# Sliding-window attention into soft-MoE on one core: masks and value order moved to TensorE, 128-key tiles with halos, longer weight rows

## The chip, the cores and the metric

One core of one Trainium2 chip. The metric is the time of one execution on the device in microseconds, the median of the runs. Everything that is called busy, waiting or a clock below is read from the profiles of single executions; the span of a profile is about 1.8 us shorter than the measured time of the same run. "Full" and "half" clock are the two rates that the clock records of the TensorE show (1.00 and 0.50).

## The reference, cut to what matters

```python
# q, k, v: (8 batches, 8 heads, 576 tokens, 64), fp32
scores = q @ k.T / 8
rel = pos[:, None] - pos[None, :]
mask_plain = (rel >= 0) & (rel < 32)                        # heads 0..3
mask_dil   = (rel >= 0) & (rel < 128) & (rel % 4 == 0)      # heads 4..7
attn = softmax(where(mask, scores, -1e9));  o = attn @ v
x = o.transpose(0, 2, 1, 3).reshape(4608, 512)
logits = x @ phi                                            # phi: 512 x 32 slots
d = softmax(logits, axis=0);  slot_in = d.T @ x             # sums over all 4608 rows
slot_out[e] = relu(slot_in[e] @ w1[e]) @ w2[e]              # 8 experts, 2 + 2 MB each, fp32
out = softmax(logits, axis=1) @ slot_out
```

The sum over all rows splits the work in two. No expert product can start before the last batch's attention is done; the weights can be loaded under the attention.

## The kernel before

Eight batches run in a software pipeline. Each has six score tiles (`kt` 0 to 5): TensorE computes them, ScalarE takes the exponent, VectorE multiplies by a 0/1 mask, and eleven output tiles follow. Values of the plain heads arrive in six overlapping tiles of 96 new keys; dilated heads use tokens sorted by residue modulo 4.

```python
def load_v(b):                       # 128-byte pieces (64 fp16) for the plain heads
    nc.gpsimd.dma_start(out=vt[32:128, :, :, 0:D],
        in_=v[b, 0:4].rearrange("h (t a) d -> a (h t) d", t=NT))
    ...                              # dilated heads: 512-byte rows into a stage, then ScalarE copies

def emit_scores(b, kt):
    ...
    for kt_, k0, qt_, q0, c0, w in jobs:
        for tt in range(2):
            for hh in range(2):
                p0 = 32 * (2 * pair + hh)
                nc.tensor.matmul(sps[:, hh, c0:c0+w], kt_[p0:p0+32, k0:k0+128, tt],
                                 qt_[p0:p0+32, q0:q0+w, tt], start=(tt == 0), stop=(tt == 1))

def emit_mask(b, kt):                # six a batch, on VectorE
    nc.vector.tensor_tensor(out=pt[:, :, 0:n], in0=pt[:, :, 0:n],
        in1=m[:, None, :].broadcast_to([128, 2, n]), op=ALU.mult)
# ... cut: emit_av (11 tiles, two PSUM buffers), transposes of x, logits, slot sums
# after the last batch: hps = siTm x w1 (64 products), hT, so = hTm x w2 (64), 36 output tiles
```

The softmax here doesn't subtract the row's maximum and nothing guards it: scores larger than these inputs give would overflow.

## Time and profile before

| | before |
|---|---|
| median of 4 runs, us | 202.8 (202.54 to 204.49) |
| span of the profile, us | 200.8 |
| TensorE busy, VectorE busy, ScalarE busy, us | 146.6, 132.3, 100.6 |
| first score product of batches 0, 1, 2, 7, us | 9.1, 24.2, 39.2, 126.5 |
| expert products hps from, to; so from, to, us | 156.5, 162.1; 164.4, 170.7 |

These are lines of the page of the profile before. Each digit is the busy share of one fortieth of the span, in tenths (about 5 us each); GB/s is what the DMA engines moved, counted in bytes at the destination (loads as the 2-byte results of 4-byte reads, the output of the tail as 4-byte numbers); the last line is the chain of waits that ended last, by engine.

```profile
span 200.8 us, 5070 instructions
PE   0126369399889989979799998998886869758600
PEclk9999999999999999999999999955555599995555
GB/s 128 182 191 192 205 211 189 209 212 187 211 210 188 214 210 203 196 212 194 204 210 189 208 207 208 207 208 208 207 207 205 70 0 0 127 407 407 410 407 124
PE 41%; DMA 23%; ACT 10%; issue 10%; DVE 7%; POOL 6%; POOLq 0%; ACTq 0%
```

The DMA runs at about 205 GB/s until some 157 us; then the tail moves output at 407 GB/s. The dips to 187 to 194 are single slices. And TensorE is nearly as busy as the DMA from 45 us on. The view by windows has it for 40 to 149 us (columns: window, its length, then busy us and count of PE, PEld, DVE, ACT, POOL, then clock, DMA share, GB/s):

```profile
40.00:149.00 109.00, 98.18 (x1555) 66.96 (x1553) 87.19 (x250) 67.04 (x104) 28.95 (x37) 0.91 1.29 204
```

TensorE works for 98.18 of 109 us, 90%, against 80% for VectorE.

The PEclk row needs care: the records of this execution begin at 126.4 us, and the row prints 9 before that for want of a record. These groups of products by form in one batch (73 to 92.1 us) show the real clock. The columns are line, engine, operation, output and inputs, shapes, count, busy us, mean ns of one, idle time before.

```profile
L360 PE MATMUL lg_0_1329<-xTd_1277,phi_61 128*128 128x288 f16 x2 | 0.8, 418 | 0.0
L342 PE MATMUL rd_0_1629<-ident,xd_1439 128*128 128x128 f16 x5 | 1.1, 303 | 0.0
```

In the same trace the last two of a run of 128-column transposes start 106 or 107 ns apart (those before them 79 to 92), and 96-column ones 79 or 80. That is one column in 0.83 ns, half clock.

### The profile page before, as it was taken

The page shows a single profiled execution, that of the slowest core. Times are in us where ns is not written, and L with a number is a line of the kernel's source. Part 1 is how long each engine was busy: PE and PEld are TensorE (multiplying, and loading weights), DVE is VectorE, ACT ScalarE, POOL GpSimd, SP SyncE. Part 2 cuts the span into 40 slices and gives each one's busy share as a digit, 9 for nine tenths or more (in the row PEclk, how much of TensorE's full clock was granted, in tenths as well). Part 3 has the DMA queues.
Part 4 walks back from the last instruction along what each step waited for, and adds up shares of the span by engine and source line. Part 5 has one row for each costly group of instructions (what it writes and reads, how often), then busy time and mean ns, then how long its engine had stood idle before and what let it go on. Part 6 is the DMA issues. An engine that isn't in the chain of part 4 may idle for free.

```text
span 200.8 us, 5070 instructions
## 1 busy us (share of the span) xinstructions
PE 146.6 (73%) x2128; PEld 91.8 (46%) x2128; DVE 132.3 (66%) x354; ACT 100.6 (50%) x150; POOL 66.9 (33%) x102
## 2 busy tenths in 40 slices
PE   0126369399889989979799998998886869758600
PEld 0115256158647746646465675675655344211000
DVE  3688697678896998597779678986632120755520
ACT  2037448384872963595386675565433020655510
POOL 7736224215215403501750003055000000598850
PEclk9999999999999999999999999955555599995555
DMA  6999999999999999999999999999999400499994
GB/s 128 182 191 192 205 211 189 209 212 187 211 210 188 214 210 203 196 212 194 204 210 189 208 207 208 207 208 208 207 207 205 70 0 0 127 407 407 410 407 124
DMA packets 46422, 40.99 MB, mean 204 GB/s; under 512 B 20672, under 2 KB 33600, under 8 KB 46400
## 3 DMA queue, kind: packets, MB, share of 16 engines
q0 software_dynamic: 46112, 40.41, 117.0%
q8 instruction: 16, 0.26, 0.5%
q1 hardware_dynamic: 288, 0.27, 0.4%
q14 instruction: 6, 0.05, 0.1%
HBM read 62.20 MB, written 9.44 MB: 357 GB/s over the span
## 4 chain that ended last, share of the span: by engine, by line
PE 41%; DMA 23%; ACT 10%; issue 10%; DVE 7%; POOL 6%; POOLq 0%; ACTq 0%
DMA v_93<-in_v_dram 10%; DMA vsa_1638<-in_v_dram 8%; DMA vsa_148<-in_v_dram 5%; PE so L597 3%; POOL out_dram L621 3%; ACT ET L363 3%; PE hps L563 3%; DVE qk_89 L200 1%; ACT v_92 L174 1%; PE lg_0_977 L360 1%; PE s_4_1993 L238 1%; PE lg_0_1329 L360 1%; PE lg_0_2031 L360 1%; PE lg_0_626 L360 1%; POOL raw_0_121 L150 1%
## 5 line engine op out<-in xcount | busy, mean ns | idle before, releaser
L238 PEld LDWEIGHTS <-qk_89 32*128 32x128 f16 x448 | 14.1, 116 | 22.3 <-DVE qk_89 L200 10.5
L238 PEld LDWEIGHTS <-qk_90 32*128 32x128 f16 x448 | 14.4, 113 | 10.3 <-issue 5.1
L621 POOL DMA_DIRECT2D out_dram<-ot_3191 x1 | 0.6, 561 | 33.4 <-ACT ot_3191 L616 33.4
L360 PEld LDWEIGHTS <-phi_61 128*128 128x128 f16 x64 | 7.6, 128 | 8.1 <-issue 3.5
L613 PEld LDWEIGHTS <-ET 128*128 128x128 f16 x36 | 3.6, 99 | 14.3 <-issue 13.0
L238 PE MATMUL s_0_178<-qk_89 32*128 32x96 f16 x12 | 0.7, 270 | 9.1 <-DVE qk_89 L200 9.1
L193 POOL DMA_DIRECT2D w_5_2337<-in_moe_w_dram x1 | 0.9, 873 | 18.0 <-PE o_0_2311 L273 18.0
L580 ACT ACTIVATE h_sb<-hps 128x512 f16<-128x512 f32 x1 | 0.6, 598 | 9.8 <-PE hps L563 9.8
L605 DVE CAST so_sb<-so 128x256 f16<-128x256 f32 x1 | 0.4, 425 | 6.8 <-ACT so_sb L604 6.8
L581 DVE TENSOR_SCALAR h_sb<-hps 128x512 f16<-128x512 f32 x1 | 0.7, 692 | 6.3 <-ACT h_sb L580 6.3
L251 ACT ACTIVATE pa_0_191<-s_0_178 128x576 f16<-128x576 f32 x1 | 0.7, 651 | 7.8 <-PE s_0_178 L238 7.8
L374 PEld LDWEIGHTS <-ET 32*128 32x128 f16 x48 | 1.9, 99 | 5.5 <-ACT ET L363 5.5
L238 PE MATMUL s_2_214<-qk_89 32*128 32x96 f16 (+2 forms) x28 | 1.1, 215 | 4.3 <-DVE qk_89 L209 3.7
L405 PEld LDWEIGHTS <-ones 96*128 96x128 f16 x48 | 4.0, 103 | 0.0
L563 PEld LDWEIGHTS <-siTm 128*32 128x32 f16 x64 | 2.1, 128 | 4.1 <-issue 2.5
L563 PE MATMUL hps<-w_0_76,siTm 128*32 128x512 f16 x8 | 3.2, 548 | 1.0 <-DVE siTm L549 1.0
L193 POOL DMA_DIRECT2D w_7_2689<-in_moe_w_dram x4 | 2.8, 707 | 3.1 <-PE o_0_2663 L273 2.9
L157 POOL DMA_DIRECT2D v_92<-in_v_dram x3 | 3.6, 1195 | 0.7 <-DMA raw_0_121<-in_q_dram 0.7
L200 DVE STREAM_TRANSPOSE qk_89<-raw_0_121 128x576 uint32<-128x576 uint32 x1 | 1.3, 1256 | 3.9 <-DMA raw_0_121<-in_q_dram 3.9
L184 DVE COPY v_93<-v_93 32x1280 f16<-32x1280 f16 x2 | 1.0, 484 | 4.2 <-DMA v_93<-in_v_dram 4.2
L157 POOL DMA_DIRECT2D v_91<-in_v_dram x3 | 3.6, 1209 | 0.0
L391 DVE TENSOR_TENSOR er_2948<-ep_2933,emask 128x352 f16<-128x352 f16 x1 | 0.3, 342 | 4.9 <-PE ep_2933 L384 4.9
(1047 smaller groups left out, 614.0 us busy)
## 6 DMA issues: line engine op xcount, KB each, us to landing
w_0_76<-in_moe_w_dram POOLq DMA_DIRECT2D x1, 1024.0 KB, 18.6
w_1_77<-in_moe_w_dram POOLq DMA_DIRECT2D x1, 1024.0 KB, 18.6
w_2_78<-in_moe_w_dram POOLq DMA_DIRECT2D x1, 1024.0 KB, 14.8
w_3_79<-in_moe_w_dram POOLq DMA_DIRECT2D x1, 1024.0 KB, 13.5
w_4_80<-in_moe_w_dram POOLq DMA_DIRECT2D x1, 1024.0 KB, 17.7
w_5_81<-in_moe_w_dram POOLq DMA_DIRECT2D x1, 1024.0 KB, 16.0
w_6_82<-in_moe_w_dram POOLq DMA_DIRECT2D x1, 1024.0 KB, 13.4
w_7_83<-in_moe_w_dram POOLq DMA_DIRECT2D x1, 1024.0 KB, 18.5
```

The costliest lines, as they stand in the source:

```text
L150: nc.gpsimd.dma_start(out=t[:, g, :], in_=ten[b, 4 * g : 4 * g + 4].rearrange("h (p j) d -> (h p) (j d)", j=PJ),)
L157: nc.gpsimd.dma_start(out=vt[32:128, :, :, 0:D], in_=v[b, 0:4].rearrange("h (t a) d -> a (h t) d", t=NT))
L193: nc.gpsimd.dma_start(out=w2t[e][:, n * i : n * i + n, :], in_=src[:, n * i : n * i + n, :])
L200: nc.vector.transpose(out=dst, in_=src)
L238: nc.tensor.matmul(sps[:, hh, c0 : c0 + w], kt_[p0 : p0 + 32, k0 : k0 + 128, tt], qt_[p0 : p0 + 32, q0 : q0 + w, tt], start=(tt == 0), sto ...
L360: nc.tensor.matmul(lp, phi4[:, kc].rearrange("p c s -> p (c s)"), rhs, start=(kc == 0), stop=(kc == 3))
L363: nc.scalar.activation(out=ET[:, b * S : b * S + S].rearrange("p (i r) -> p r i", r=DIL)[:, 2 * rp : 2 * rp + 2, :], in_=lp, func=AF.Exp, ...
L405: nc.tensor.matmul(up[:, c, :], l, rr, start=(i == 0), stop=(i == len(jobs) - 1), skip_group_check=True)
L563: nc.tensor.matmul(hps[32 * j : 32 * j + 32, fc, :], siTm[:, dc, e, :], w1t[e][:, dc, 512 * fc : 512 * fc + 512], start=(g == 0 and dc == ...
L597: nc.tensor.matmul(so[32 * j : 32 * j + 32, :], hTm[g][:, c, 32 * j : 32 * j + 32], w2t[4 * g + j][:, c, :], start=(g == 0 and c == 0), st ...
L613: nc.tensor.matmul(fp, ET[:, r0 : r0 + 128], so_sb, start=True, stop=True)
L621: nc.gpsimd.dma_start(out=out[r0 : r0 + 128, :], in_=ot)
```

## The change

Its intent is to unload VectorE and ScalarE, to give the DMA longer rows, and to keep the array busy with useful work:

- The mask is added before the exponent: a product of the identity with a bias tile (0 or -30000) opens each score tile. Twelve such products a batch, 5376 columns; the six VectorE mask products go.
- Keys are in tiles of 128, with query windows of 160 (plain) and 144 (dilated). Queries that reach back into the tile before get a second, 32-by-32 product from it, a halo: 32 a batch.
- Values arrive four tokens to a row. One-hot products (24 a batch, 256 columns each) put them in order, and VectorE evicts the result three times a batch. GpSimd copies the values of the dilated heads.
- The values of the last 64 tokens of all batches are loaded in one go at the start (`vleft`).
- Weight rows are 8 KB (w1) and 16 KB (w2) of input instead of 4 KB and 2 KB.
- 24 products on zeros warm the array; the outputs use one PSUM buffer of two banks.

```diff
-def make_masks():   # 0 / 1
+def make_bias():    # 0 / -30000
@@ load_v
-            out=vt[32:128, :, :, 0:D], in_=v[b, 0:4].rearrange("h (t a) d -> a (h t) d", t=NT)
+            out=st, in_=v[b, :, 0:512, :].rearrange("h (a r) d -> a h (r d)", r=DIL)
+    def load_vleft():
+        for b in range(B):
+            nc.gpsimd.dma_start(out=vleft[16 * b : 16 * b + 16],
+                in_=v[b, :, 512:576, :].rearrange("h (a r) d -> a h (r d)", r=DIL))
+    def permute_v(b, part):            # one-hot products, then an eviction
+            for u in range(2):
+                t = 2 * part + u
+                for r in range(DIL):
+                    nc.tensor.matmul(pv[:, u], sel[:, 128 * t + 3 - r : 128 * t + 131 - r],
+                        st[:, 0:4, D * r : D * r + D], start=(r == 0), stop=(r == DIL - 1))
... (part 2: the same for vleft)
+        nc.vector.tensor_copy(out=dst, in_=pv)
@@ load_w1, load_w2
-  moe_w1[e].rearrange("(c p) f -> p c f", p=128)
+  moe_w1[e].rearrange("(g p c) f -> p g (c f)", g=2, c=2)
-  moe_w2[e].rearrange("(c p) f -> p c f", p=128)
+  moe_w2[e].rearrange("(p c) f -> p c f", c=8)
@@ emit_scores
+        for hh in range(2):
+            nc.tensor.matmul(sps[:, hh, 0:n] ..., ident, <bias tile>, start=True, stop=False)
... (then the score products with start=False)
-    def emit_mask(b, kt): ...
@@ emit_av: two output tiles a group, products "mains" of 128 keys, then "halos"
+                        halos.append((slice(o0, o0 + 32), h, hl, vp[96:128, u - 1, h]))
+            jobs = mains + halos
... (cut: strides of the transposes of x, warm-up, the order of loads)
+N_WARM = 24
```

## The prediction

> **What bounds the kernel now.** Loads. The table of slices shows the DMA over 90% busy from 5 to 155 us at 187 to 214 GB/s of 2-byte results (62.2 MB are read as 4-byte numbers, so about twice that), and the last weight lands near 157 us. Behind it comes a serial tail: in the chain of waits the expert products hps run 156.5 to 162.1, so 164.4 to 170.7, then 36 stores at 407 GB/s; the span ends at 200.8, so 30.1 us after so. Attention takes about 17 us a batch (the first score products of batches 3 to 7 start at 57, 73, 90, 107 and 126 us) and ends at 154.4, level with the loads.
>
> **A hidden cost: the matrix clock.** The table prints clock 1.00 until 126 us, but that is only a lack of records. In the timeline 128-column transposes start 106 ns apart and 65-column products 54 ns apart: half clock, by the two rates that the Trainium skill gives (TensorE: Matmul & The Clock Gate, "Wait — 56ns, not 53.3ns?": 107 against 56 ns). From 160.5 to 181 us, 512-column products start 215 ns apart: full clock. Adding up columns weighted by the share of array rows and columns used, in the 3.41 us steps of the clock records, I estimate that the clock rose after windows at 0.39 and 0.50 of the full rate and fell after 0.23 and 0.25. Attention averages about 0.27, so it stays at half clock.
>
> **What the change does, per batch.**
> - VectorE loses 6 mask products (0.45 to 0.68 us each) and the value shifts (0.5 + 0.4), merges 11 normalisations into 5, and gains 3 evictions of about 0.7 us: about 15 to 12.5 us.
> - ScalarE loses two 1.05 us copies (one goes to GpSimd), and gains 15% of exponent columns: about 11.5 to 10 us.
> - TensorE gains 12 identity products (5376 columns), 24 one-hot products (some 5400) and 32 small halo products: 240 to 290 products. My estimate of its array time is 11.4 us before at half clock; after, 21 us at half or 10.5 us at full clock. The weighted use after would be 9 us of full rate per batch, 0.6 of a 15 us batch, above what raised the clock. The 24 warm-up products start it high. I expect mostly full clock.
> - DMA: 128-byte value rows become 512-byte ones, weight rows 2 to 8 times longer. The dips to 187 GB/s should nearly go: 6 us less load time. Three fewer first-layer weights go ahead of the last batch's values, so attention may run ahead of the weights.
>
> **Critical path.** If a batch takes 14 to 15 us, attention ends near 140 us, hps leaves the path, and what stays is loads to about 152 us, the last eight so products (3.4 us at half clock), and the unchanged 30 us: 186 us of span, 188 us measured with the 1.8 us by which the median exceeds the span. Each microsecond of batch time above 14.4 delays the loads by about 5 us, since they wait for staging buffers; at 17 us all gain is gone.
>
> **Predicted: 188 us, 182 to 198 (8 in 10). Faster by over 2%: 0.86; within: 0.07; slower: 0.07.**
>
> **What would show it.** Transposes 53 to 60 ns apart and full clock in most attention windows; score starts 14 to 15 us apart; no dips below 200 GB/s; hps finished 5 us or more before the last weight lands; VectorE busy near 110 us.
>
> **What would make it wrong.** The clock falling back (21 us a batch, some 225 us); the two-buffer PSUM ring, now taking 11 tiles a batch instead of 8, or the single output buffer stalling the in-order TensorE; GpSimd's copies holding up load issue, leaving gaps in the DMA rows.

## The result and the profile after

The kernel after takes 211.76 us (median of 4 runs, 211.28 to 212.46) against 202.8 us before. The ratio is 1.0419, with a 95% interval of 1.0368 to 1.0469: slower, outside the predicted range. All ratios here are the mean time of one kernel's fast runs over that of the other's in the same rounds, so they are not quite the ratio of the medians.

The lines of the page after that answer to those of before:

```profile
span 210.1 us, 5705 instructions
PE   7959749989999998998998998998856869768600
PEclk9967979999999999999999999999655599995555
GB/s 107 194 159 161 202 207 209 208 212 209 210 211 207 202 150 208 178 106 204 219 74 210 216 222 218 212 215 218 211 220 201 9 0 3 51 408 409 407 409 113
PE 60%; ACT 11%; DVE 10%; issue 7%; DMA 4%; POOL 4%; POOLq 0%; ACTq 0%
```

How to read the difference: the chain of waits has moved from the DMA (23% to 4%) to TensorE (41% to 60%). VectorE's busy time fell from 132.3 to 106.8 us, TensorE's rose from 146.6 to 172.7 us. The clock record now begins at 5.2 us and is real: full from 32.5 to 148.5 us. The same view by windows as before has TensorE at work for 103.55 of 109 us, 95%:

```profile
40.00:149.00 109.00, 103.55 (x1853) 69.43 (x1850) 62.44 (x124) 68.53 (x95) 23.98 (x33) 1.00 1.05 196
```

Three slices of the GB/s row drop deeply (150, then 178 and 106, then 74).

The starts of the batches' first score products show where the time went (after the change the first product of a score tile is its bias product; lengths are taken before rounding):

| us | before | after | change of the stretch |
|---|---|---|---|
| batch 0 | 9.1 | 8.4 | |
| batch 2 | 39.2 | 49.2 | start: +10.7 |
| batch 7 | 126.5 | 133.3 | five batches: 87.3 to 84.2, -3.1 |
| hps | 156.5 | 165.4 | last batch and drain: 30.0 to 32.0, +2.0 |
| end of the span | 200.8 | 210.1 | tail: 44.3 to 44.7, +0.4 |

A batch fell from 17.5 to 16.8 us, where 14 to 15 had been predicted, and the start lost more than five batches gained. The tail is unchanged, as predicted.

The same groups of products after, in one batch (66.11 to 82.87 us), against the lines of before above: the logits take 286 ns instead of 418, the transposes 222 instead of 303, at the same shapes. In the trace, transposes start 56 ns apart instead of 106. The clock did double. So the matrix clock, rival C below, is not what keeps these batches long.

```profile
L396 PE MATMUL lg<-xT,phi 128*128 128x288 f16 x8 | 1.5, 286 | 0.7 <-ACT xT L383 0.7
L379 PE MATMUL rg<-ident,x 128*128 128x128 f16 x8 | 0.8, 222 | 0.0
```

So why does a batch still take 16.8 us? These are all the waits of TensorE in that batch (view of waits; columns: us in total, times, longest):

```profile
PE lg L396 <- ACT xT L383: 0.7, 1, 0.7
```

TensorE waits for others for 0.7 us of 16.8. It is the bound itself. By start-to-next-start times in this batch, by use, against what I had estimated from the columns alone, with products on different parts of the array taken as overlapping:

| products in a batch | estimate, us at full clock | measured, us |
|---|---|---|
| bias | 2.25 | 2.84 |
| scores | 2.2 | 4.52 |
| probabilities times values, with halos | 1.25 | 2.91 |
| one-hot | 2.25 | 2.71 |
| transposes of x | 1.0 | 1.48 |
| logits | 0.96 | 1.01 |
| slot rows and sums | 0.6 | 1.32 |
| sum | 10.5 | 16.8 |

Of the 6.3 us between the sums, 3.6 are the changes of tile shape that come next, 0.7 is the wait above, and 1.9 lie in products that follow each other less closely than their columns allow, 0.7 of them in the value products with their halos.

This stretch of the timeline shows one reason (start us, busy us, what, count):

```profile
69.61 0.28 PE L342 MATMUL o<-v,pb 128*128 128x65 f16 x4
69.73 0.53 PE L269 MATMUL s<-bias,ident 128*128 128x432 f16 x2
70.19 0.80 PE L285 MATMUL s<-qk 32*64 32x64 f16 x28
```

From four value products to the bias products both use the whole array; the four take 0.12 us, 30 ns each. The two bias products of 432 columns start at 69.73 and need 2 x 182 ns, so they are done streaming at about 70.09; the score products on 32 rows of the array start at 70.19, a tenth of a microsecond later, and nothing is waited for. Over all batches from 49 to 150 us there are 38 such changes of the array's tile shape in a batch. Each costs a median of 96 ns beyond the columns streamed (middle half: 93 to 98 ns), 3.6 us a batch. Where one group of products that use the whole array follows another such group, the median is 12 ns. Before the change there are 27, at a median of 125 ns at half clock.

The Trainium skill says in "TensorEngine Tiling (Array Packing)", section "Key Properties", that changing the tiling mode drains the TensorE. It gives no figure; this trace shows a cost there and puts 96 ns on it, without showing what it is made of.

The halos are the second reason. These are instruction starts from the trace after (us, then ns since the product before), four halos of plain heads and four of dilated ones:

```
71.152 122      71.614 124
71.192  40      71.617   3
71.228  36      71.620   3
71.257  29      71.623   3
```

The four dilated halos use the same 32 rows and four different 32-column places of the array and start 3 ns apart, as the skill has it ("TensorE: Matmul & The Clock Gate", sections "The mechanism" and "Measured speedup vs the span model": tiles at different positions overlap, with starts about 4 ns apart). The sixteen halos of plain heads share one place in each group of four, and follow each other at 29 to 40 ns. I had costed all of them as if they overlapped. By these spacings that is an estimated 0.4 us a batch, much less than the changes of shape; and the first of each group pays such a change.

### The profile page after: what moved, and what is told of

Read it like the earlier page. It is cut to its first block, busy times and chain, and to the rows that moved or that the text cites. A ratio compares the mean times of both kernels' runs of the same rounds, so it can differ in the third digit from the quotient of the medians.

```text
span 210.1 us, 5705 instructions
## 1 busy us (share of the span) xinstructions
PE 172.7 (82%) x2552; PEld 104.4 (50%) x2552; DVE 106.8 (51%) x209; ACT 96.2 (46%) x134; POOL 61.3 (29%) x99
## 4 chain that ended last, share of the span: by engine, by line
PE 60%; ACT 11%; DVE 10%; issue 7%; DMA 4%; POOL 4%; POOLq 0%; ACTq 0%
PE s L285 12%; PE o L342 11%; PE pv L186 8%; ACT xT L383 6%; DMA vs<-in_v_dram 4%; PE s L272 4%; PE lg L396 4%; PE u L444 4%; PE s L269 3%; PE rg L371 3%; PE so L644 3%; POOL out_dram L668 3%; ACT pc L299 3%; PE hps L610 3%; DVE qk L232 2%
## 5 line engine op out<-in xcount | busy, mean ns | idle before, releaser
L285 PE MATMUL s<-qk 32*32 32x16 f16 (+3 forms) x832 | 35.9, 210 | 4.3 <-DVE qk L232 4.1
L285 PEld LDWEIGHTS <-qk 32*128 32x128 f16 (+2 forms) x832 | 22.0, 93 | 26.5 <-issue 19.7
L212 DVE CAST v<-pv 128x512 f16<-128x512 f32 x24 | 16.4, 688 | 28.7 <-PE pv L204 18.0
L174 POOL COPY v<-vs 128x1024 f16<-128x1024 f16 x8 | 8.4, 1046 | 75.7 <-PE o L342 56.8
L668 POOL DMA_DIRECT2D out_dram<-ot x36 | 19.0, 533 | 36.6 <-ACT ot L663 34.6
L352 DVE TENSOR_TENSOR x<-o,rc 128x512 f16<-128x512 f32 x40 | 27.4, 685 | 1.0
L299 ACT ACTIVATE pa<-s 128x960 f16<-128x960 f32 x16 | 15.4, 970 | 25.8 <-PE s L285 25.7
L232 DVE STREAM_TRANSPOSE qk<-raw 128x576 uint32<-128x576 uint32 x16 | 19.3, 1233 | 6.5 <-PE s L285 3.2
L186 PE MATMUL pv<-vs,sel 128*128 128x256 f16 x128 | 19.8, 307 | 2.6 <-DMA vs<-in_v_dram 2.4
L383 ACT COPY xT<-rg 128x512 f16<-128x512 f16 x16 | 20.8, 1310 | 0.2 <-PE rg L382 0.2
L241 DVE STREAM_TRANSPOSE qk<-raw 128x320 uint32<-128x320 uint32 (+1 forms) x32 | 19.7, 662 | 0.3 <-DMA raw<-in_q_dram 0.2
L660 PE MATMUL f<-so_sb,ET 128*128 128x512 f16 x36 | 14.4, 452 | 4.1 <-DVE ot L665 2.1
L272 PE MATMUL s<-bias,ident 128*128 128x480 f16 (+1 forms) x64 | 17.4, 356 | 0.0
```

The lines of the kernel that those rows point to most:

```text
L186: nc.tensor.matmul(pv[:, u], sel[:, 128 * t + 3 - r : 128 * t + 131 - r], st[:, 0:4, D * r : D * r + D], start=(r == 0), stop=(r == DIL - 1),)
L212: nc.vector.tensor_copy(out=dst, in_=pv)
L232: nc.vector.transpose(out=dst, in_=src)
L241: nc.vector.transpose(out=o, in_=i)
L272: nc.tensor.matmul(sps[:, hh, 0:n].rearrange("p (t i) -> p t i", t=3), ident, win[:, None, 0:w].broadcast_to([128, 3, w]), start=True, sto ...
L285: nc.tensor.matmul(sps[m if isinstance(m, slice) else slice(0, m), hh, c0 : c0 + w], l, r, start=False, stop=(tt == 1 and ji == len(jobs) ...
```

## The experiments

Theory A: the batch is bound by one in-order chain on TensorE, and what it costs beyond the columns is the changes of tile shape. Rival B: the loads, held back behind GpSimd's copies (the prediction had named this). Rival C: the matrix clock. All kernels below gave correct results. "Batch" is the time from one batch's first score product to the next.

### Is it TensorE or the loads?

**e1, fewer changes of shape.** Value products of two output tiles are issued first and their halos after them; short transposes and slot sums use all 128 rows.

```diff
-            jobs = mains + halos
-            for i, (ps, h, l, rr) in enumerate(jobs):
-                nc.tensor.matmul(...)
+            allmains += ...;  allhalos += ...
+        for uu, ps, h, l, rr, first, last in allmains + allhalos:
+            nc.tensor.matmul(...)
-            n0 = 64 if u == 4 else 0
+            n0 = 0          # rows 0..63 of that tile weighted by zero
```

> Same work, nine fewer changes of array shape per batch (38 to about 29): the products of both halves of an output group are ordered by shape, and the two transposes and the slot sums of the last 64 tokens use all 128 rows. Theory A (the in-order TensorE binds attention even at full clock, and each change of array shape costs 96 ns, as the trace of the changed kernel shows): 0.86 us less per batch, 6 to 8 us less in all, about 204 to 206 us. Theory B (loads held back by the GpSimd copies bind): no change, 211 us, within 1 us.

Measured 208.38 us, ratio 1.0263 (1.0200 to 1.0325). The changes fell to 29 a batch, and undisturbed batches to 16.2 us from 16.8 (one took 16.5, one 17.0): 0.6 us for nine changes, about 70 ns each where 96 had been reckoned. The whole is 3.4 us less than after, in the direction of A but short of the expected 204 to 206.

**e2, GpSimd's copy behind the loads.**

```diff
-            if att and kt == 2 and b + 1 < B:
-                spread_v_dil(b + 1)
+            if kt == 2 and 0 < b < B - 1:
+                for e in (b,) if b < B - 2 else (b, b + 1):
+                    spread_v_dil(e)
```

> The GpSimd copies of the strided values move behind the loads of two batches ahead, so that loads no longer wait for an output product. Theory B: the gaps in the DMA rows near 73, 90 and 107 us (some 8 us of lost transfer) vanish and the time falls by 5 to 8 us. Theory A: the gaps vanish or shrink, the weights land earlier, but the expert products start as late as before, and the time stays within 1.5 us of 211.8.

Measured 211.21 us, ratio 1.0385 (1.0300 to 1.0471). First what GpSimd's queue waited for after the change, then the GB/s row of e2.

```profile
POOL v L174 <- PE o L342: 56.8, 5, 12.8
```

```profile
GB/s 102 197 161 164 204 207 209 206 215 208 212 209 208 214 207 210 212 210 212 213 218 223 210 218 162 218 213 218 215 104 0 3 0 3 48 408 407 408 409 114
```

After the change the copies wait 56.8 us in total for the output products of TensorE, with the loads queued behind them. In e2 the three deep drops are gone (one slice of 162 is left), and the last weight lands at 156.7 us instead of 164.3. The batch is 16.8 us as before, hps starts at 165.3 instead of 165.4, and the time is within the scatter of after. Rival B is refuted: the gaps are real and cost nothing, because the loads have slack behind TensorE.

**e3, the bias products twice.** The same values are added a second time, which changes no masked result.

```diff
-        for hh in range(2):
+        for rnd, hh in ((0, 0), (0, 1), (1, 0), (1, 1)):
...
-                    start=True,
+                    start=(rnd == 0),
```

> Every identity product of the mask bias is run twice (adding minus 60000 instead of minus 30000; the result is the same). 12 products more per batch, 5376 columns, 2.24 us at full clock, 17.9 us over eight batches. Theory A (TensorE binds): 15 to 18 us more, 227 to 230 us. Theory B (loads bind, TensorE has slack): under 5 us more. The clock should stay full, since the array is used more.

Measured 222.75 us, ratio 1.0929 (1.0835 to 1.1023). The batch grew by 1.7 us to 18.5 us for 2.24 us of added columns, and hps came 11.8 us later, at 177.1. So three quarters of the time added on TensorE lengthened the batch: it is on the path. But the total, 11 us more than after, missed the 227 to 230 of A. (The profile is slow by its time, with the clock full from 41 to 164 us, so the batches are those of full clock.)

### The start

**e4, no warm-up.** One product on zeros instead of 24 (`N_WARM = 1`).

> 1 warm-up product instead of 24. The trace of the changed kernel shows that the full clock it won was lost at 12 us anyway and won again by the attention itself at 18.8 and for good at 32.5 us. So I expect no more than 2 us either way, and the full clock from about 33 us on. If the warm-up is what holds the clock, the attention stays at half clock and the time rises by 30 us or more.

Measured 213.78 us, ratio 1.0520. The clock went full on its own at 17.4 us and held from 34.5 to 150.5 us. The warm-up is worth about 2 us, and is not what holds the clock high.

**e5, the last values with each batch.** `vleft` is loaded per batch, the queries and keys of batch 1 come earlier, and the one-hot products of batch 1 move into batch 1.

```diff
-    load_vleft()
-    nc.gpsimd.dma_start(out=phi_raw, ...)
     load_qk(0, 1)
     load_qk(1, 1)
+    nc.gpsimd.dma_start(out=phi_raw, ...)
@@ in load_v
+        nc.gpsimd.dma_start(out=vleft[b], in_=v[b, :, 512:576, :]...)
-            if b == 0 and kt in (1, 2, 3): permute_v(0, kt - 1)
-                    if b == 0: ... permute_v(1, part)
+            if b == 0 and kt in (2, 3, 4): permute_v(0, kt - 2)
+            if b == 1 and kt < 3: permute_v(1, kt)
```

> Only the start is changed: the values of the last 64 tokens come with each batch instead of all eight batches before batch 1's queries and keys, and the first one-hot products stand later in TensorE's order. In the changed kernel batch 1's first complete scores wait until 29.0 us (24.2 before), and batch 2 starts at 49.2 (39.2 before). Theory: the start costs 5 to 10 us of the loss, since everything after it is one TensorE chain; so batch 2 starts at 40 to 44 us, the batch time stays at 16.8 us, and the whole is 204 to 207 us. If the start is hidden by a later limit: no change, 211 us.

Measured 215.23 us, ratio 1.0549, a clear miss. Batch 1 started at 25.0 us and batch 2 at 51.0 instead of 49.2. The clock was half from 24.6 to 34.9 and from 38.3 to 45.1 us, where after it was half for only 3.4 us in that stretch. The lower clock may have taken what the order gained; no run separates the two.

### Taking work off TensorE

**e6, plain values in order by DMA.** Rows of one token again, so that 16 of 24 one-hot products and two of three evictions go.

```diff
+        for h in range(4):
+            nc.gpsimd.dma_start(out=vP[b % 4][:, :, h, 0:D],
+                in_=v[b, h, 0:512, :].rearrange("(t a) d -> a t d", a=128))
-            out=st, in_=v[b, :, 0:512, :]...
+            out=st, in_=v[b, 4:8, 0:512, :]...
@@ permute_v
-        if part < 2: ... (16 one-hot products)
+        if part < 2: return
```

> The plain heads' values of the first 512 tokens come straight from the DMA in key order, in runs of 64 numbers as before the change, so 16 of the 24 one-hot products and two of three evictions per batch fall away. TensorE theory: 1.75 us less per batch (16 products 109 ns apart), 10 to 13 us in all, 199 to 202 us. DMA theory (short runs are what hurt): the dips of the kernel before come back, loads end later and the time does not fall, or rises.

Measured 210.01 us (207.08 to 215.97), ratio 1.0194 (1.0127 to 1.0261), not the 199 to 202 expected. The profile is slow: batches of 15.4 us at full clock, and of 19.8 and 21.4 us in a stretch from 51.2 to 82.0 us at half clock. The start did gain: batch 2 began at 42.7 us instead of 49.2, with the same wait of 4.0 us for batch 1's queries. The dips to 188 GB/s came back, as the other theory had it, but the last weight landed at 164.0 us, against 164.3 after.

**e7, everything at once.** The edits of e1, e2, e5 and e6, and one strided ScalarE eviction a batch moved to VectorE.

> Fewer shape changes, late copies, the new load order, values by DMA, and one of the two strided evictions of the dilated half on VectorE, all together. TensorE theory: 16.8 - 0.8 - 1.75 - 0.6 gives 13.5 to 14.5 us per batch, batch 2 starts near 41 us, attention ends near 140 us; then the end of the loads (150 to 154 us), the last second-layer products and the 30 us of stores remain: 186 to 192 us, faster than both kernels. If something else binds, it stays above 198 us.

Measured 208.88 us (204.06, 205.75, 212.01, 214.96); fast runs against fast runs 1.0056 (0.9983 to 1.0130). The profile is fast:

```profile
span 202.3 us, 5487 instructions
PE   7929999998999999898998998998757969768600
PEclk9965555698555555999999999999855599995555
```

Batches 4 to 6 take 14.4, 14.4 and 14.2 us, just what the prediction had said, though with 16 one-hot products a batch fewer than it counted, so the agreement is luck. Batches 1 to 3 take 19.7, 21.0 and 19.6 us, in the stretch where PEclk is 5 (half from 11.8 to 39.1 and from 49.3 to 80.0 us). Batch 2 began at 44.1 us. Both stretches run the same program, with TensorE busy 100% of the time at half clock (49.3 to 80.0 us) and 93% at full clock (80.0 to 144.9). So at this amount of work either clock holds itself. My estimate of the use, columns weighted by the share of array rows and columns they occupy, is about 6.8 us of full-rate work a batch: 0.34 of a 20 us batch, 0.47 of a 14.4 us one. In the kernels before and after, a 3.41 us step was followed by full clock when its use was above about 0.39 and by half clock when it was below about 0.35; these two values lie on either side. Counted the same way over all fifteen traces, 240 of 241 steps below 0.35 were followed by half clock and all 468 above 0.42 by full; between the two both occur (95 full, 39 half). Plain columns, not weighted by the share of the array, do not sort the steps like this. The steps are estimates (a few per cent of the product records can be missing), and the rule is a fit, not something the profile prints.

**e8, the kernel before with useless products.** Twelve identity products a batch are written into the score tiles and then overwritten.

```diff
+        for hh in range(2):
+            nc.tensor.matmul(sps[:, hh, 0:n], ident, masks[:, 0:n], start=True, stop=True)
```

> The kernel before, with two useless identity products ahead of each score tile (12 per batch, 4672 columns, overwritten by the scores), only to use the array more. By my threshold estimate the weighted use rises from 0.27 to about 0.4 to 0.45 of full rate, so the clock should rise in most of attention: 128-column transposes 56 ns apart instead of 106. If half clock was a cost to the kernel before, it gets faster by over 2% in spite of the added work; if its loads bound it, it stays within 2%: I expect 199 to 204 us. If the clock does not rise: 210 us or more.

Measured 205.35 us, ratio 1.0065 (1.0018 to 1.0113). Useless work did raise the clock of the old kernel in parts (full from 73.5 to 90.5 and from 131.5 to 148.6 us, among shorter stretches, in a profile that is slow by its time), and in all it bought nothing.

**e9, four of six masks back on VectorE**, as a product after the exponent; only the mixed tiles keep their bias products.

```diff
-            else:
-                nc.tensor.matmul(sps[...], ident, win[...], start=True, stop=False)
+                        start=(kind != 1 and tt == 0),
+    def emit_mask(b, kt):
+            nc.vector.tensor_tensor(out=p4, in0=p4, in1=keep[...], op=ALU.mult)
```

> The changed kernel with the mask of four of the six score tiles per batch (the plain and the first three strided ones) applied on VectorE after the exponential, as before the change, instead of by identity products: 8 products (2688 columns) per batch less for TensorE, 4 products of about 0.6 us more for VectorE. TensorE theory at full clock: 1.1 to 1.5 us less per batch, 15.3 to 15.7 us, 201 to 205 us. But the clock theory warns: the weighted use per batch falls from about 9 to 7.9 us of full rate; at full clock that is 0.5 of a batch, above the 0.38 at which the steps of the records change the clock, so I expect most of attention at full clock, yet some low stretch early on as in the runs with fewer products; if half of the batches run at half clock, 207 us or more.

Measured 208.12 and 209.22 us in the fast runs, 217.19 and 219.19 in the slow ones; fast 1.0256. In the profiled fast run the batch is 15.9 us and the clock is full from 33.5 to 135.9 us only. By the start of the batches' first score products that is 0.9 us a batch less than after, but hps came at 162.4 us, only 3.0 us earlier. Batch and time both missed the range expected for TensorE at full clock.

### Holding the clock

**e10, e7 with filling products** (useless identity products in the first four batches) and **e11, the same with filling in the later batches too**, more PSUM for the last batch's outputs and one memset on GpSimd.

```diff
+        for hh in list(range(2)) * ({(0, 2): 8, (1, 0): 6}.get((b, kt), 1 if 0 < b < 4 else 0)):
+            nc.tensor.matmul(sps[:, hh, 0:NB], ident, bias[:, 0:NB], start=True, stop=True)
```

> All mends together as in the earlier run of that name (batches of 14.4 us at full clock, but 20 us while the clock sat at half from 12 to 39 and from 49 to 80 us), and now useless identity products in the first four batches only: 16 before the third score tile, 12 before batch 1, 2 per score tile in batches 1 to 3. Clock theory: more work in the array holds the clock, batches 1 to 3 take 16 to 17 us instead of 20 to 21 and the rest 14.4, so 12 to 15 us are won against that run's profiled 202 us of span: 188 to 194 us, and the runs agree within 2 us instead of 11. If the clock has nothing to do with the use of the array, the added work (4 us or more at half clock per batch) makes it slower: 212 us or more.

> As the run with early filling, with two more filling products per batch in the two weakest score tiles of batches 4 to 7 (0.7 us a batch), and a shorter end of attention: two PSUM buffers more for the last batch's outputs and the clearing of a late buffer on GpSimd instead of VectorE. If the early filling is enough to hold the clock, the late filling costs 3 us of attention and the shorter end wins 2 to 3, so about equal, 188 to 194 us; if the clock still falls in batches 4 to 7 without it, this one wins by 4 us or more.

e10: 208.29 us median of six. The mean clock and the time of each run, from its own records: 0.878 with 199.35 us, 0.842 with 207.94, 0.841 with 206.53, 0.819 with 208.89, 0.818 with 208.65, 0.811 with 209.93. One program on one chip: with less full clock it takes longer, by and large. Only the fastest run is a fast one, so there is no ratio, and one run at 199.35 proves no version better. e11: 205.46 us, ratio 1.0016 (0.9961 to 1.0071). In its profile, of a slow run, a batch that fell in a spell at half clock from 122.5 to 139.6 us took 19.3 us, the one before it 15.5. Both missed their range: with filling, spells of half clock remained.

**e12, keep all products, cut only changes of shape and waits**: after, with the edits of e1 and e2, and one strided eviction moved:

```diff
-            nc.scalar.copy(
+            (nc.scalar.copy if kc == 2 else nc.vector.tensor_copy)(
                 out=dst[:, 0:512].rearrange("p (i r) -> p r i", r=DIL),
```

> The kernel after, with the reordering of e1 (fewer changes of array tile shape), the late GpSimd copy of e2, and one of the two strided ScalarE evictions of each batch moved to VectorE; the one-hot and identity products all stay, so the array keeps its use. If the full clock is what the work products buy, it holds from about 32 to 148 us here as it does after the change, and the batch falls from 16.8 to about 15.5 us (1.0 from the switches, 0.3 to 0.7 from the wait on the eviction): 202 to 206 us. If the clock falls in attention as it did in e6, e7 and e9, 208 or more.

Measured 205.48 us (204.95 to 205.58, the tightest of all variants), ratio 1.0093 (1.0038 to 1.0149).

```profile
span 203.8 us, 5711 instructions
PEclk9979957999999999999999999999965599995555
```

The clock held from 33.0 to 149.1 us, as after. The time fell by 6.3 us in all, within the expected 202 to 206. Batches took 16.1 us in quiet stretches, not 15.5 (one took 16.5, one 17.1). Of the 6.3 us, 1.1 are before batch 2 (48.0 us), 2.3 in the next five batches and 2.9 in the last batch and drain (29.1 us instead of 32.0). Against e7 this is the plain comparison: e7 has less work and an unsteady time, e12 has more work and a steady one.

**e13, e12 with batch 1's queries and keys loaded first** and its one-hot products spread.

```diff
     load_v(0)
+    load_qk(0, 1)
+    load_qk(1, 1)
     load_vleft()
     nc.gpsimd.dma_start(out=phi_raw, ...)
-    load_qk(0, 1)
-    load_qk(1, 1)
```

> As e12, with the queries and keys of batch 1 loaded ahead of the last-64-token values of all batches, and the one-hot products of batch 1 spread through batch 1. If the late load and the one-hot products in a row cost the start 4 to 7 us at full clock, batch 2 starts at 43 to 45 us, not 49, and the whole takes 197 to 201 us. If the array, emptied of those products, falls to half clock in the first 45 us, batch 2 starts near 49 as before and nothing is gained on e12.

Measured 207.31 us (205.56 to 215.05), ratio 1.0163 (1.0091 to 1.0236). Batch 2's first score product stands at 42.5 us, but TensorE did other work in the middle of that tile, and the second tile began at 49.4 us (49.8 in e12):

```profile
42.46 0.57 PE L272 MATMUL s<-bias,ident 128*128 128x480 f16 x2
49.43 0.36 PE L272 MATMUL s<-bias,ident 128*128 128x480 f16 x1
```

Batch 3 began at 64.8 us (64.1 in e12): no gain. The two waits that answer each other, first TensorE's in e12, then those of TensorE, VectorE and GpSimd's queue in e13, from 8 or 5 to 50 us:

```profile
PE s L285 <- DVE qk L232: 4.1, 1, 4.1
```

```profile
PE o L345 <- DVE v L212: 4.1, 1, 4.1
DVE qk L232 <- DMA raw<-in_q_dram: 7.3, 2, 4.2
POOL raw L149 <- DVE qk L241: 10.9, 2, 10.4
```

In e12 the scores of batch 1 wait 4.1 us for VectorE's transposes of its queries. In e13 these transposes come earlier in VectorE's order and wait 4.2 us there for their data, with the eviction of the values behind them, and TensorE waits 4.1 us for that eviction. The wait moved and kept its size. The clock was half from 17.7 to 24.6 us.

## Why the prediction was wrong

- **"TensorE ... My estimate of its array time is ... 10.5 us at full clock" and "If a batch takes 14 to 15 us".** This is the step that failed. The mechanism (more array use, full clock) came true; the array's time was mis-sized, because columns were added up as if shapes could follow each other freely. Measured: 16.8 us a batch, 6.3 more, of which 38 changes of tile shape are 3.6 us, a wait 0.7, and the rest mostly short products that start no closer than some 25 to 40 ns, the halos of plain heads among them. e1 and e12 show that fewer changes shorten the batch at unchanged clock; that the 96 ns is a drain is the skill's word, and no run here separates it from another cost of the change.
- **The start was not in the sum at all.** Batch 2 starts 10.0 us later than before. For 4.1 us, until 29.03, TensorE waits for batch 1's queries, whose loads were issued at 14.5 us instead of 6.7 and 8.0; batch 0 waits 2.4 us for values; the clock is half for 10 us of the first 33; and batch 1's one-hot products run in a row. TensorE's waits in that stretch (8 to 50 us), longest first:

```profile
PE s L285 <- DVE qk L232: 4.1, 1, 4.1
PE pv L186 <- DMA vs<-in_v_dram: 2.4, 1, 2.4
```

The trace shows these parts; how much each costs is not shown. e4, e5 and e13 changed the warm-up and the order, and none gained. What did gain is less work: without 16 of the 24 one-hot products a batch, batch 2 began 6.5 us earlier in e6 and 5.0 in e7, so in e6 6.5 of the 10.0 us lost at the start went with these products and the 2.4 us wait for their values. TensorE is busy for 32.9 us between the starts of batches 0 and 2 after the change, against 15.9 before.
- **How the sum came out.** I had expected hps to be free near 140 us; it began at 165.4. With 14.5 us a batch from 8.4 us, batch 2 would have begun at 37.4 and batch 7 at 109.9 us. The start is 11.8 us of the difference, the five batches 11.7 us, the last batch and drain 1.9 us.
- **"What bounds the kernel now. Loads."** Half right. Before the change the loads last about as long as attention: hps begins at 156.5 us, and the last weight lands at 159.7, 4.7 us before so begins. But the TensorE is 90% busy from 40 to 149 us at half clock, so it was level with the loads, and it is the one the change loads further. After the change loads have slack (e2). The prediction's own warning, that at 17 us a batch all gain is gone, came out nearly right, but not by its mechanism, delayed loads: in e2 the last weight lands 7.6 us earlier and hps starts at 165.3 us all the same.
- **"I expect mostly full clock."** Right: full from 32.5 to 148.5 us. The fall-back to 21 us a batch did not occur in the kernel after. It occurred in e6 and e7, which do less work.
- **DMA dips.** Right for rows: the weights alone move at 210 to 222 GB/s after, 207 or 208 before. The named risk of GpSimd's copies came too, with three deep gaps, and cost nothing (e2).
- **VectorE about 110 us, tail unchanged.** Right: 106.8 us; 44.7 us of tail against 44.3. The ring of two PSUM buffers and the single output buffer, also named as risks, hold TensorE up by nothing visible in a steady batch.

So the expected gain went three ways: the doubled clock was spent on 20% more products and their changes of shape, five batches gained 3.1 us in all, and the start gave 10 us back. No variant clearly beats both kernels: e11 (1.0016) and e7 (1.0056) are level with before, and e12 is the steadiest. What stays open: what the first 49 us need, and whether a version with batches of 14.4 us that stays at full clock throughout would come near 188 us. e10's single run at 199.35 us, at the largest share of full clock of its six, hints at it and doesn't show it.

## What to carry to other kernels

Cost a TensorE stream by start-to-start times, with a charge for every change of tile shape (here 96 ns, 38 a batch), and group products of one shape before counting columns; small products only overlap where they sit on different places of the array. When a busy kernel runs at half clock, useful array work can buy the full one, but then taking work away again can lose it: measure the clock with every such edit. Before moving work onto an engine, ask whether it is off the path in every stretch, the first batches included.

## What the Trainium skill lacked or had wrong

- "TensorEngine Tiling (Array Packing)", "Key Properties", says that a change of tiling mode drains the TensorE and gives no time. Here: median 96 ns at full and 125 ns at half clock, 38 and 27 times a batch.
- "TensorE: Matmul & The Clock Gate", "What's actually happening", lists the throttled state as idle or cold and the full one as busy or warm after one sustained window. Here the kernel before ran at half clock with TensorE about 90% busy from 40 to 126 us (by the spacing of its transposes), and e7 ran the same program at both clocks for 30 us and more (19.6 to 21.0 against 14.2 to 14.4 us a batch). What sorted the steps in all fifteen traces was the share of the array used in a 3.41 us step: by my estimate below 0.35 of the full rate half clock followed (240 of 241), above 0.42 full clock (468 of 468).
- The same page, "Part 4: PE-mode transpose", says that the full clock doesn't engage for transposes and gives about 275 ns for each in one kernel. Here, among other products, they do run at either clock: 56 ns apart and 222 ns long at full clock, 106 ns apart and 303 ns long at half. Whether transposes alone would raise the clock no run here shows.
- No page that I read says that such a half-clock state can hold itself by making the work slower and so the array less used; e7 shows both states in one run, at 20 and 14.4 us a batch.
